# An attention and MLP kernel: the attention exps in two phases on either side of w3, the second q/k tile filled by DMA, all engine orders pinned

## The chip, the cores and the metric

The kernel runs on one core of one Trainium2 chip. The metric is device time in microseconds (us) of one execution; lower is better. Most executions of one kernel agree within 0.3%, but several kernels here fall into two groups about 2% apart, fast or slow (slow: more than 1.5% above the fastest of the same kernel), and comparisons use fast runs. The profile also gives the *granted clock* of TensorE: 1 is full speed, 0.5 is half.

A *ratio* in this text is the estimate of one kernel's time over that of the kernel before, from the fast runs of the same rounds on the same chip. It is not quite the ratio of the medians quoted beside it. Brackets give a 95% interval.

## The reference, cut to what matters

```python
# S = 2048 positions, D = 512, 32 heads of 16, F = 1376, bf16
x = A_x
xn = layernorm(x)
# A: each query sees 8 keys: itself and those 2, 4, ... 14 positions back
s = attention(xn @ wqkv, window=8, dilation=2) @ wo
# B: h = gelu(layernorm(xn) @ w1); its four column groups shifted by +1, -1, +2, -2 rows; then w2
x1 = xn + shifted(h) @ w2
b  = x1 + gelu(layernorm(x1) @ w3) @ w4
out = x + s * silu(b)
```

Positions fall into an even and an odd half (p = 0 and p = 1) of 1024; dilation 2 makes attention a dense window of 8 inside a half. Each half has nine *units* of up to 128 queries.

## The kernel before

The sliding window is imposed inside the score matmul. A score matmul reads 32 rows (partitions) of a key tile and of a query tile: 16 rows are one head, and 16 rows are *mask rows*, whose product adds a large negative number outside the window. Two tiles exist of each (e = 0 and 1), in which heads and mask rows change places. ScalarE writes the q/k rows into both tiles from the matmul's result, and then DMAs overwrite 16 of every 32 rows of each tile with mask rows out of a small table in memory.

```python
for a in range(ND):                             # stage_a2: QK
    ...                                         # 8 matmuls into pt
    for e in range(2):                          # the result goes into both tiles
        nc.scalar.activation(dst[e][:, n0 : n0 + 2, cs], pt, AF.Copy)

for w in range(2):                              # end of build_mask: the table goes to memory
    nc.sync.dma_start(out=mask_d[w].rearrange("r (g l) -> g r l", l=W), in_=rows[w])

def fill_mask(p, w):                            # w: 0 keys, 1 queries
    t = (kT[p], qT[p])[w]
    for e in range(2):
        for gr in range(4):
            r = 32 * gr + DH * (1 - e)          # 16 partitions, 128 KB
            pin(nc.sync.dma_start(out=t[e][r : r + DH, :, :],
                                  in_=mask_d[w].unsqueeze(1).to_broadcast([DH, ND, M])))
```

(`DH` is 16, `ND` 4, `M` 1024, and `pin` keeps an instruction in program order.) `nc.sync` is the queue of the SyncE engine, the only one that issues loads here. Each entry waits for what it needs; entries behind it wait with it. The order of the stages is:

```python
stage_ln(0) ... stage_a2(2)        # layer norm, transposes, QK and w1 of four chunks of 512
build_mask()
stage_b(0); stage_a2(3); stage_b(1); stage_b(2)   # w2, third layer norm, round trip through memory
stage_w3(0); stage_b(3)
fill_mask(0, 0); fill_mask(0, 1)
stage_w3(1); stage_w3(2); stage_w3(3)
# then 18 units of attention; each holds 11 w4 matmuls in its first eight,
# the rest of w4 and wo tiles later
```

`stage_b` ends with the *round trip*: the normalised x1 goes to memory and comes back transposed as `x1nT`, which w3 reads. After every third unit comes the chain of the *denominators*: the sums of the exps go to memory, come back (`dn`), VectorE takes the reciprocal (`rb`), it goes to memory (`rden_d`) and comes back spread out, and VectorE multiplies the attention output by it.

The softmax here doesn't subtract the row's maximum and nothing guards it: scores larger than these inputs give would overflow.

## Time and profile before

227.31 us, median of 3 runs (226.96 to 228.37).

| what | before |
|---|---|
| span of the profiled execution | 222.8 us |
| PE (TensorE matmul) busy | 205.6 us, 92% |
| ACT (ScalarE) busy | 136.2 us |
| first QK matmul | 10.06 us |
| waits for mask rows, 110 to 114 us | 3.1 us in four pieces |
| a unit of attention with 11 w4 matmuls | 4.78 us |

The following lines are from the page of the kernel before. The rows of digits cut the span into 40 slices of 5.6 us; each digit is the busy share (or, for PEclk, the granted clock) in tenths. The last line is the chain of work that ended last, by engine.

```profile
span 222.8 us, 4851 instructions
PE 205.6 (92%) x1992; PEld 95.3 (43%) x1992; DVE 130.1 (58%) x244; ACT 136.2 (61%) x158; POOL 61.9 (28%) x119
PE   8799999999999999999869999999969999999961
PEclk9999999999999999999988999999999999999998
DMA  5999100130390675799995005526650342625222
PE 67%; DMA 10%; DVE 8%; ACT 7%; POOL 2%; SPq 2%; issue 2%; DVEq 0%; ACTq 0%
```

TensorE is busy nearly everywhere. Two dents are visible before the end: one in the slices of 107 to 118 us, where the clock falls too, and a 6 in the slice of 161 to 167 us. DMA is 10% of the chain. The next lines are pieces of that chain (start, us, what):

```profile
97.31 7.99 DMA kT_155<-mask_d
105.32 8.73 DMA qT_159<-mask_d
```

And these are lines of TensorE's timeline there (start, us, engine, line, operation, tiles; in brackets the idle time just before and what ended it):

```profile
110.69 0.21 PE L461 MATMUL s_ps<-qT_159,kT_155 32*128 32x128 bf16 x1 [0.47 <-DMA qT_159<-mask_d]
111.90 0.21 PE L461 MATMUL s_ps<-qT_159,kT_155 32*128 32x128 bf16 x1 [0.99 <-DMA qT_159<-mask_d]
112.89 0.21 PE L461 MATMUL s_ps<-qT_159,kT_155 32*128 32x128 bf16 x1 [0.67 <-DMA qT_159<-mask_d]
114.08 0.21 PE L461 MATMUL s_ps<-qT_159,kT_155 32*128 32x128 bf16 x1 [0.98 <-DMA qT_159<-mask_d]
114.34 3.24 PE L413 MATMUL w_ps<-w_sb,h3T 128*128 128x512 bf16 x9
120.47 2.12 PE L413 MATMUL w_ps<-w_sb,h3T 128*128 128x512 bf16 x9
```

Four groups of scores wait for the four mask transfers one by one. Then nine matmuls take 3.24 us; nine at the full clock, 6 us later, take 2.12. (A duration shown here includes the end of the pipeline; the matmuls themselves follow each other every 0.2156 us.)

### The profile page before, as it was taken

Reading aid. Unit: us, or ns where it says so; the run is one execution under the profiler, and the core shown is the slowest. Engines: PE = TensorE matmul, PEld = TensorE weight load, DVE = VectorE, ACT = ScalarE, POOL = GpSimd, SP = SyncE. Lnnn points to the kernel's source line nnn. Section 1 sums busy time; section 2 is a strip of 40 time slices with the busy share of each in tenths; the row PEclk is TensorE's granted clock in tenths of the full one; section 3 lists DMA queues with packets and bytes.
Section 4 is the critical chain, followed back from the end, with each engine's and each line's share of the span. In section 5 each row is a group of like instructions: output and inputs, shape, how many; then the busy total and the mean of one; then the engine's idle time right before and its main releaser. Section 6 shows DMA issues by size and latency. Waiting matters only on the chain.

```text
span 222.8 us, 4851 instructions
## 1 busy us (share of the span) xinstructions
PE 205.6 (92%) x1992; PEld 95.3 (43%) x1992; DVE 130.1 (58%) x244; ACT 136.2 (61%) x158; POOL 61.9 (28%) x119
## 2 busy tenths in 40 slices
PE   8799999999999999999869999999969999999961
PEld 2335545444444444444323444444434445454420
DVE  6689964127279683000103566678457857795984
ACT  2086696956913615665457888898776978842110
POOL 1723563502002202000000007015074482947040
PEclk9999999999999999999988999999999999999998
DMA  5999100130390675799995005526650342625222
GB/s 160 371 392 388 47 0 4 4 8 0 122 161 3 171 195 154 170 118 121 119 122 60 0 3 119 157 68 159 209 125 13 101 83 70 154 51 148 67 85 94
DMA packets 32957, 25.60 MB, mean 115 GB/s; under 512 B 16152, under 2 KB 28792, under 8 KB 32936
## 3 DMA queue, kind: packets, MB, share of 16 engines
q1 hardware_dynamic: 30312, 22.16, 42.7%
q0 software_dynamic: 1536, 2.10, 4.9%
q10 hardware_dynamic: 1088, 1.05, 1.3%
q8 instruction: 15, 0.25, 0.5%
q14 instruction: 6, 0.05, 0.1%
HBM read 16.58 MB, written 4.52 MB: 95 GB/s over the span
## 4 chain that ended last, share of the span: by engine, by line
PE 67%; DMA 10%; DVE 8%; ACT 7%; POOL 2%; SPq 2%; issue 2%; DVEq 0%; ACTq 0%
PE w_ps L413 17%; PE qk_ps L317 9%; PE w_ps L392 9%; ACT prob L468 6%; PE w_ps L329 6%; PE w_ps L357 6%; PE s_ps L461 5%; PE v_ps L440 5%; PE wo_ps L573 4%; DMA qT_159<-mask_d 4%; DMA kT_155<-mask_d 4%; PE o_ps L489 3%; DVE l1s L253 2%; SPq L224 2%; DMA oT_1494<-orw 2%
## 5 line engine op out<-in xcount | busy, mean ns | idle before, releaser
L468 ACT ACTIVATE prob<-s_ps 128x960 bf16<-128x960 f32 (+2 forms) x72 | 62.7, 925 | 15.1 <-PE s_ps L461 14.1
L413 PE MATMUL w_ps<-w_sb,h3T 128*128 128x512 bf16 (+1 forms) x176 | 44.9, 390 | 0.0
L392 PE MATMUL w_ps<-x1nT,w_sb 128*128 128x512 bf16 (+1 forms) x176 | 38.3, 379 | 0.0
L397 ACT ACTIVATE h3T<-w_ps 128x1024 bf16<-128x1024 f32 x20 | 20.5, 1024 | 25.6 <-PE w_ps L392 23.3
L521 POOL DMA_DIRECT2D oT_1494<-orw x24 | 12.4, 523 | 68.2 <-DVE orw L496 68.2
L392 PEld LDWEIGHTS <-w_sb 128*128 128x128 bf16 (+1 forms) x176 | 17.6, 100 | 20.4
L413 PEld LDWEIGHTS <-h3T 128*128 128x128 bf16 (+1 forms) x176 | 15.1, 99 | 17.3 <-issue 1.0
L496 DVE CAST orw<-o_ps 128x960 bf16<-128x960 f32 (+2 forms) x18 | 19.7, 1098 | 1.3 <-PE o_ps L489 1.1
L445 DVE CAST v_aug_148<-v_ps 128x512 bf16<-128x512 f32 (+1 forms) x9 | 6.1, 682 | 23.0 <-PE v_ps L440 23.0
L317 PEld LDWEIGHTS <-wqk_sb 128*128 128x128 bf16 x128 | 12.1, 98 | 12.9
L317 PE MATMUL qk_ps<-xnT_152,wqk_sb 128*128 128x512 bf16 x64 | 15.3, 379 | 0.8 <-DVE xnT_152 L291 0.8
L420 DVE TENSOR_TENSOR xn_95<-w_ps,xn_95 128x512 bf16<-128x512 f32 x8 | 5.5, 684 | 16.5 <-PE w_ps L413 16.5
L329 PE MATMUL w_ps<-xn2T,w_sb 128*128 128x512 bf16 x64 | 14.6, 379 | 0.0
L317 PE MATMUL qk_ps<-xnT_153,wqk_sb 128*128 128x512 bf16 x64 | 14.5, 379 | 0.0
L584 POOL TENSOR_TENSOR xo_1715<-sg,xo_1715 128x512 bf16<-128x512 bf16 x8 | 10.4, 1297 | 14.5 <-DVE sg L582 13.4
L362 DVE TENSOR_TENSOR xn_95<-w_ps,xn_95 128x1024 bf16<-128x1024 f32 x4 | 4.9, 1215 | 14.4 <-PE w_ps L357 14.4
L422 ACT ACTIVATE sig<-xn_96 128x512 bf16<-128x512 bf16 x8 | 5.0, 630 | 12.6 <-DVE xn_96 L420 12.6
L521 POOL DMA_DIRECT2D oT_2418<-orw x24 | 12.1, 513 | 1.6 <-DVE orw L496 1.6
L246 POOL TENSOR_SCALAR l3r<-l3m 128x4 f32<-128x4 f32 x4 | 0.9, 232 | 36.7 <-DVE l3m L254 36.7
L440 PE MATMUL v_ps<-wv_sb,xnT_153 128*128 128x512 bf16 (+1 forms) x36 | 9.3, 380 | 2.0 <-DVE sg L582 2.0
L461 PE MATMUL s_ps<-qT_159,kT_155 32*128 32x120 bf16 (+2 forms) x144 | 7.7, 214 | 3.1 <-DMA qT_159<-mask_d 3.1
L573 PE MATMUL wo_ps<-wo_sb,oT_2418 128*128 128x512 bf16 x32 | 7.6, 379 | 2.2 <-DVE oT_2418 L545 2.2
(132 smaller groups left out, 329.3 us busy)
## 6 DMA issues: line engine op xcount, KB each, us to landing
w_sb<-in_B_w_dram SPq DMA_DIRECT2D x1, 1376.0 KB, 9.5
w_sb<-in_B_w_dram SPq DMA_DIRECT2D x1, 1280.0 KB
wqk_sb<-in_A_wqkv_dram SPq DMA_DIRECT2D x2, 512.0 KB
w_sb<-in_B_w_dram SPq DMA_DIRECT2D x2, 512.0 KB, 6.0
xn_96<-in_A_x_dram SPq DMA_DIRECT2D x4, 256.0 KB, 6.9
xo_1715<-in_A_x_dram SPq DMA_DIRECT2D x4, 256.0 KB, 5.5
xo_2325<-in_A_x_dram SPq DMA_DIRECT2D x4, 256.0 KB, 4.5
out_dram<-xo_1715 SPq DMA_DIRECT2D x4, 256.0 KB, 3.8
```

The lines of the kernel that those rows point to most:

```text
L317: nc.tensor.matmul(pt[:, b, :], lhsT=wqk_sb[:, dt, nt * P : (nt + 1) * P], rhs=xnT[p][:, dt, cs], start=(dt == 0), stop=(dt == ND - 1),)
L329: nc.tensor.matmul(pt[:, b, :], lhsT=w1_sb[:, dt, g * P : (g + 1) * P], rhs=xn2T[:, dt, :], start=(dt == 0), stop=(dt == ND - 1),)
L357: nc.tensor.matmul(pt[:, j, :], lhsT=w2_src(p, g, m0), rhs=w2_sb[:, g, :], start=(g == 0), stop=(g == ND - 1),)
L392: nc.tensor.matmul(pt[:fs, ft % 2, :], lhsT=w3_sb[:, dt, ft * P : ft * P + fs], rhs=x1nT[:, dt, :], start=(dt == 0), stop=(dt == ND - 1),)
L397: last["gelu"] = nc.scalar.activation(h3T[:, 2 * a : 2 * a + 2, :], pt, AF.Gelu_apprx_tanh)
L413: nc.tensor.matmul(pt, lhsT=h3[c][:fs, ft, jj * P : (jj + 1) * P], rhs=w4_sb[:fs, ft, :], start=(ft == 0), stop=(ft == NF - 1),)
L440: nc.tensor.matmul(vp[:nk, :], lhsT=xnT[p][:, dt, k0 : k0 + nk], rhs=wv_sb[:, dt, :], start=(dt == 0), stop=(dt == ND - 1),)
L461: nc.tensor.matmul(st[:nk, b, i * nq : (i + 1) * nq], lhsT=kT[p][e][r : r + 32, dt, k0 : k0 + nk], rhs=qT[p][e][r : r + 32, dt, q0 : q0 + ...
L468: nc.scalar.activation(prv[:nk, 2 * h : 2 * h + 2], st[:nk, :, 0 : 4 * nq], AF.Exp, scale=SCALE)
L496: nc.vector.tensor_copy(out=orw[p][:, :, :, q0 - ra : q0 - ra + nq], in_=op[:, :, 0 : 4 * nq].rearrange("p j (s q) -> p j s q", q=nq),)
L521: nc.gpsimd.dma_start(out=oT[p][DH * hh : DH * (hh + 1), :, ra : ra + rw], in_=orw[p][32 * cg : 32 * cg + DH, jj],)
L573: nc.tensor.matmul(pt[:, j, :], lhsT=oT[p][:, dt, (i + j) * P : (i + j + 1) * P], rhs=wo["sb"][:, dt, :], start=(dt == 0), stop=(dt == ND ...
```

## The change

Its intent is to spread ScalarE's exps, and to start attention earlier. The even half's nine units move in front of w3 (*phase 1*), interleaved with QK of the odd half and with w2; the odd half's nine units stay behind w3 (*phase 2*), interleaved with w4; all wo tiles go to the end. ScalarE no longer writes the second q/k tile; a DMA called `spread` copies the 16 head rows from tile 0 to tile 1 (partition to partition), and the mask rows of tile 0 can be filled only after it. The w4 load moves into the w3 stage. All five engines run in program order. The diff also puts nearly all tiles into one arena, halves the first layer norm's statistics and loads x ahead of w1, among other things. The core of the diff:

```diff
-            for e in range(2):
-                nc.scalar.activation(dst[e][:, n0 : n0 + 2, cs], pt, AF.Copy)
+            nc.scalar.copy(out=dst[:, n0 : n0 + 2, k * CH : (k + 1) * CH], in_=pt)
...
+    def spread(p, w):
+        t = (kT[p], qT[p])[w]
+        for gr in range(4):
+            r = 32 * gr + DH
+            nc.sync.dma_start(out=t[1][r : r + DH, :, :], in_=t[0][r : r + DH, :, :])
...
+    ctx.enter_context(tc.manual_schedule(engines={E.PE, E.Activation, E.DVE, E.Pool, E.SP}))
...
     build_mask()
+    for w in range(2):
+        fill_mask(0, w, 1)               # mask rows of tile 1: 8 transfers of 128 KB
...
+    for w in range(2):                   # after QK of chunk 1
+        spread(0, w)                     # 4 copies of 128 KB
+        fill_mask(0, w, 0)               # then 4 fills of tile 0
...
+    for n in range(N1):                  # phase 1: units of p = 0 with QK of p = 1 and w2
+        attend(n)
+    for c in range(NCH):                 # w3
+        for a in range((NF + 1) // 2):
+            w3_pair(c, a)
+            if c == 0 and a == 0:
+                weighted(*prev)()
+                prev = None
+                ln3_stats(2)
+                ln3_norm(2)              # round trip of chunk 2
+                ln3_stats(3)
+                ln3_norm(3)              # round trip of chunk 3
+                for w in range(2):
+                    spread(1, w)
+                    fill_mask(1, w, 0)
+                load_w4()
+                pack(0, 2)
+            if c == 1 and a == 0:
+                normalise_end(0, 1)
+                normalise_mid(0, 2)
+            if c == 2 and a == 0:
+                normalise_end(0, 2)
...
+    for n in range(N1, 2 * NU):          # phase 2: units of p = 1 with w4
+        attend(n)
```

## The prediction

> **What bounds the kernel now.** TensorE, and time in which it is starved. The page shows PE busy 205.6 of 222.8 us and PE as 67% of the chain that ended last. A full 128x512 matmul costs 0.2156 us of stream (timeline: 16 in 3.45 us); 744 of them are 160 us. Transposes add 3.5, 36 score groups about 18 (0.5 each), 18 weighted groups 9.5 (0.53 each): about 192 us that neither kernel avoids. The other 31 us are start (first QK matmul at 10.1), a hole at 16 to 17, and three places:
> - the mask fills: the chain has 16.7 us of mask DMA before the first exps; PE waits from 110 to 114, then runs at granted clock 0.5 to 0.7 (115 to 119 us; nine w4 matmuls take 3.2 us instead of 1.9);
> - the change of phase at 154 to 170 (exps, then the oT packing DMA, 3.55 us in the chain);
> - the end: last wo matmul at 216.4, end 222.8.
>
> In the middle, a unit of attention with 11 w4 matmuls takes 4.78 us, which is its PE work. ACT has 3.8 us of exps there (four of 0.967) and little else, but is idle half of the w3 stage.
>
> **What changes.**
> - PE work: the same matmuls, other order. No gain by itself.
> - ACT: 16 second q/k copies of 1.05 us go (17 us), none on the chain. Transpose evictions move to it (about 5 us). Two more table loads (1.28 us each).
> - DMA: 16 partition-to-partition copies, 2 MB. Fills of 512 KB take 4.39 us each now (119 GB/s, DMA share 1.1). The Trainium skill, "SBUF — State Buffer", Door 1, says DMA rate depends on the ports that the partitions reach; 16 partitions reach 4 of 16, an estimate of 109 GB/s from its 435. The trace agrees roughly.
> - Phase 1 (9 units, with 48 QK and 64 w2 matmuls): PE about 5.0 us a unit, ACT 3.9 + 0.8 of copies = 4.7. Coupled through two score banks: I expect 5.1 to 5.4.
> - Phase 2: 11 w4 matmuls a unit, 4.8 to 5.0. The wo tiles go to the end, where PE stays fed.
>
> **Sum (estimates from those durations).** First QK matmul about 8.3 (halved stats, x before w1). Then 36.5 of PE to the first scores, so about 45.5. Mask: rows ready about 24, then DMA fill 8.8, spread and fill of k, spread and fill of q, 13.5 to 17.5 more: ready 48 to 53. So PE waits 3 to 7 us again, now near 46, and pays about 1.5 of low clock. Phase 1: 47. w3: 38 + 1.5 for table loads. Phase 2: 45. Tail of w4 and wo: 28.5. Drain: 5.5. Span about 214; time is 4.5 more than the span as now: **218.5 us**, range 210 to 228. Chances: faster 0.73, same 0.20, slower 0.07.
>
> **What would show each step.** (1) first QK before 9 us; (2) the chain passes through the mask or spread DMA near 45 to 53, with one dip of the clock; (3) phase 1 at 5.1 to 5.4 us a unit, ACT over 85% busy; (4) w3 in 38 to 40 us without gaps; (5) phase 2 at 4.8 to 5.0; (6) no hole where packing is waited for; (7) PE over 95% busy from the first exp to the last matmul.
>
> **What would make it wrong.** The wait for spread and fill being over 10 us (a slower partition-to-partition copy, a late mask build): then 225 or more. Exps, QK copies and two shared banks locking step in phase 1 at 6 us a unit: 6 us more. VectorE falling behind in phase 1 or the tail. If the DMA is hidden wholly: 211.

## The result, and the profile after

The changed kernel takes **239.84 us** (median of 4 runs, 239.33 to 241.08) against 227.47 (226.96 to 228.37) for the kernel before: ratio 1.0626 [1.053, 1.0721], slower. The predicted time was 218.5 with a range of 210 to 228. Its page, the same parts (slices of 6.0 us):

```profile
span 238.6 us, 4930 instructions
PE 208.4 (87%) x1996; PEld 98.7 (41%) x1996; DVE 133.4 (56%) x244; ACT 129.7 (54%) x158; POOL 68.3 (29%) x137
PE   8889999605999999999998996299999999999870
PEclk9999999965799999999999999779999999999995
DMA  5981499669930164444287996878003050400632
PE 46%; DMA 29%; DVE 12%; SPq 5%; issue 3%; ACT 2%; POOL 1%; DVEq 0%; POOLq 0%
```

There are now two dents in the PE row, at about 42 to 60 us and 143 to 155 us, each with a dip of the clock, and DMA is 29% of the chain. The first dent in TensorE's timeline:

```profile
54.87 0.28 PE L484 MATMUL s_ps<-arena 32*128 32x128 bf16 x1 [9.32 <-DMA arena<-mask_d]
55.88 0.58 PE L484 MATMUL s_ps<-arena 32*128 32x128 bf16 x7 [0.73 <-DMA arena<-mask_d]
56.99 0.28 PE L484 MATMUL s_ps<-arena 32*128 32x128 bf16 x1 [0.53 <-DMA arena<-mask_d]
57.55 0.58 PE L484 MATMUL s_ps<-arena 32*128 32x128 bf16 x7 [0.28 <-DMA arena<-mask_d]
```

TensorE has finished all work before the first scores at 45.5 us and then waits 10.9 us in four pieces. The chain over that time (start, us, what; the pieces between, most of which issue the transfers, are left out) tells for what:

```profile
22.01 6.50 DMA mask_d<-m_rows
29.90 6.21 DMA arena<-mask_d
36.13 9.06 DMA arena<-arena
47.43 6.24 DMA arena<-arena
53.73 3.78 DMA arena<-mask_d
```

Mask table to memory, fills of tile 1, key copies, query copies, fills: 35.5 us from end to end, one after the other. (`arena` is the name of the one large tile that holds q, k, weights and more; `arena<-arena` is `spread`.) From the issue of the first fill at 28.58 to the last landing at 57.51 the queue moved 3 x 1,048,576 bytes, which is 109 GB/s.

The windows view shows the clock. The columns are the stretch, its length, five engines' busy time with instruction counts, and then PEclk, the DMA share and GB/s:

```profile
46.00:47.00 1.00, 0.00 (x0) 0.00 (x0) 0.00 (x0) 0.68 (x1) 0.00 (x0) 1.00 0.91 186
50.00:51.00 1.00, 0.00 (x0) 0.00 (x0) 0.00 (x0) 0.00 (x0) 0.00 (x0) 0.50 0.45 57
62.00:63.00 1.00, 1.00 (x4) 0.33 (x3) 0.39 (x1) 0.00 (x0) 0.00 (x0) 0.50 1.08 135
64.00:65.00 1.00, 1.00 (x20) 0.56 (x20) 0.70 (x2) 0.49 (x1) 0.00 (x0) 1.00 1.06 133
```

The clock is halved from about 49.4 us, 3.9 us after TensorE ran dry (49.4 is worked out from the mean of 0.70 in the window from 49 to 50), and comes back at 63.1, some 5.5 us after it had work again. The twelve w2 matmuls in that stretch take 5.2 us; in e10 below, at full clock, they take 2.84.

The second dent follows w3:

```profile
147.46 0.23 PE L484 MATMUL s_ps<-arena 32*128 32x128 bf16 x1 [1.02 <-DMA arena<-mask_d]
148.33 0.56 PE L484 MATMUL s_ps<-arena 32*128 32x128 bf16 x7 [0.64 <-DMA arena<-mask_d]
149.60 0.22 PE L484 MATMUL s_ps<-arena 32*128 32x128 bf16 x1 [0.70 <-DMA arena<-mask_d]
150.35 0.38 PE L484 MATMUL s_ps<-arena 32*128 32x128 bf16 x7 [0.53 <-DMA arena<-mask_d]
153.97 5.90 PE L438 MATMUL w_ps<-arena 128*128 128x512 bf16 x16 [3.25 <-DMA arena<-in_B_w_dram]
```

Scores wait for the odd half's mask rows, then w4 waits 3.25 us for its own weights, and its first sixteen matmuls take 5.90 us; in e15 below, at full clock, they take 3.63. The chain (again with pieces left out) says why the weights are late:

```profile
118.37 2.96 DMA x1n_dram<-arena
121.35 5.88 DMA arena<-x1n_dram
132.34 5.49 DMA arena<-arena
140.64 5.64 DMA arena<-arena
146.69 0.42 SPq L143
```

L143 is the w4 load, issued at 146.69 although its target was free from about 108 us, when VectorE had last read what lay there: it stood in the one queue behind two round trips, the copies and the fills, each of which waited for the one before. The Trainium skill, "DMA: Bandwidth & Descriptors", Anatomy of one DMA, states that a semaphore wait happens on the issuing sequencer before dispatch (its section follows a DMA of GpSimd's queue, but that sentence is about the DMA engines in general); this trace, of SyncE's queue, agrees: the SyncE queue's own waits between 115 and 150 us include 6.2 us for `x1n_dram<-arena`, 6.1 for `arena<-arena` and 3.7 for `den_d<-orw`.

Stage by stage, from the timeline:

| stage | predicted | after | what differs |
|---|---|---|---|
| first QK matmul | 8.3 | 8.59 | |
| first scores could start | 45.5 | 45.5 | |
| first scores after that | +3 to 7, then about 1.5 of low clock | +9.3; all mask rows in at 57.5, clock low until 63 | first dent: phase 1 ends at 106.55 and so takes 61.0; without a dent it takes 46.5 (measured in the last version below), so the dent cost 14.5 |
| phase 1, a later unit | 5.1 to 5.4 | 5.03 | |
| w3 | 39.5 | 39.9 | |
| first w4 | no hole | hole | second dent: phase 2 takes 55.0; without a dent 45.65 (the same version), so the dent cost 9.4 |
| phase 2, one unit | 4.8 to 5.0 | 4.95 | |
| tail, drain | 28.5, 5.5 | 30.0, 7.1 | |

The two dents are 23.9 us of the 238.6. Without them the span would be about 214.7; as the 46.5 and 45.65 come from e15, whose own span is 214.7, this is a way to share out the difference and not an independent check. In w3 the match with the prediction is partly luck: 39.9 includes a wait of 1.14 us for a round trip, and e15's w3 takes 38.8, so the 1.5 us for table loads did not show. Part of the tail may be VectorE, for which TensorE waits there 0.64 and 0.66 us; that the slower gate causes these waits is not shown. The gate's `SCALAR_TENSOR_TENSOR` averages 926 ns against 685 to 691 before. The one that started at 212.58 took 1.62 us, while a GpSimd add ran from 212.51 to 213.66; it ended 0.54 us after that add. The Trainium skill, "SBUF — State Buffer", on the shared port pair, says that VectorE and GpSimd exclude each other there for a whole instruction; the trace agrees.

### The profile page after: what moved, and what is told of

Its sections match the earlier page's. It is cut to its first block, busy times and chain, and to the rows that moved or that the text cites. A ratio compares the mean times of both kernels' runs of the same rounds, so it can differ in the third digit from the quotient of the medians.

```text
span 238.6 us, 4930 instructions
## 1 busy us (share of the span) xinstructions
PE 208.4 (87%) x1996; PEld 98.7 (41%) x1996; DVE 133.4 (56%) x244; ACT 129.7 (54%) x158; POOL 68.3 (29%) x137
## 3 DMA queue, kind: packets, MB, share of 16 engines
q1 hardware_dynamic: 30760, 24.26, 46.5%
## 4 chain that ended last, share of the span: by engine, by line
PE 46%; DMA 29%; DVE 12%; SPq 5%; issue 3%; ACT 2%; POOL 1%; DVEq 0%; POOLq 0%
PE w_ps L438 14%; DMA arena<-arena 11%; PE w_ps L384 7%; PE v_ps L464 6%; PE s_ps L484 6%; PE qk_ps L348 4%; DMA arena<-mask_d 4%; PE o_ps L507 3%; PE wo_ps L585 3%; DMA mask_d<-m_rows 3%; DMA rden_d<-rb 3%; DMA arena<-x1n_dram 2%; SPq L222 2%; DMA arena<-in_A_x_dram 2%; DVE arena L591 2%
## 5 line engine op out<-in xcount | busy, mean ns | idle before, releaser
L489 ACT ACTIVATE arena<-s_ps 128x960 bf16<-128x960 f32 (+2 forms) x72 | 63.2, 934 | 27.8 <-PE s_ps L484 27.8
L438 PE MATMUL w_ps<-arena 128*128 128x512 bf16 (+1 forms) x176 | 44.2, 394 | 3.3 <-DMA arena<-in_B_w_dram 3.2
L546 POOL DMA_DIRECT2D arena<-orw x48 | 24.9, 526 | 73.5 <-DVE orw L519 62.4
L484 PE MATMUL s_ps<-arena 32*128 32x120 bf16 (+2 forms) x576 | 19.9, 213 | 14.4 <-DMA arena<-mask_d 13.8
L423 ACT ACTIVATE arena<-w_ps 128x1024 bf16<-128x1024 f32 x20 | 20.5, 1024 | 16.9 <-PE w_ps L418 16.9
L438 PEld LDWEIGHTS <-arena 128*128 128x128 bf16 (+1 forms) x176 | 17.1, 100 | 24.4 <-issue 6.7
L388 DVE TENSOR_TENSOR arena<-w_ps,arena 128x512 bf16<-128x512 f32 x16 | 11.0, 688 | 27.9 <-PE w_ps L384 27.9
L418 PEld LDWEIGHTS <-arena 128*128 128x128 bf16 (+1 forms) x176 | 17.4, 100 | 21.6 <-DMA arena<-x1n_dram 1.6
L418 PE MATMUL w_ps<-arena,arena 128*128 128x512 bf16 (+1 forms) x88 | 19.3, 379 | 1.1 <-DMA arena<-x1n_dram 1.1
L418 PE MATMUL w_ps<-arena 128*128 128x512 bf16 (+1 forms) x88 | 19.5, 379 | 0.0
L464 PE MATMUL v_ps<-wv_sb,arena 128*128 128x512 bf16 (+1 forms) x72 | 18.6, 380 | 0.2 <-DVE arena L444 0.2
L384 PE MATMUL w_ps<-arena 128*128 128x512 bf16 x64 | 18.6, 426 | 0.0
L332 PE MATMUL qk_ps<-arena 128*128 128x512 bf16 (+1 forms) x96 | 18.3, 344 | 0.0
L361 PE MATMUL w_ps<-arena 128*128 128x512 bf16 x64 | 14.5, 379 | 0.0
```

The source lines that it names most:

```text
L332: nc.tensor.matmul(pt[:, b, hh * w : (hh + 1) * w], lhsT=wqk_sb[:, dt, nt * P : (nt + 1) * P], rhs=xnT[p][:, dt, k * CH + hh * w : k * CH ...
L384: nc.tensor.matmul(pt, lhsT=w2_src(p, g, m0), rhs=w2_sb[:, g, :], start=(g == 0), stop=(g == ND - 1))
L418: nc.tensor.matmul(pt[:fs, ft % 2, :], lhsT=w3_sb[:, dt, ft * P : ft * P + fs], rhs=x1nT[c][:, dt, :], start=(dt == 0), stop=(dt == ND - 1),)
L423: nc.scalar.activation(h3T[c][:, 2 * a : 2 * a + 2, :], pt, AF.Gelu_apprx_tanh)
L438: nc.tensor.matmul(pt, lhsT=h3T[c][:fs, ft, jj * P : (jj + 1) * P], rhs=w4_sb[:fs, ft, :], start=(ft == 0), stop=(ft == NF - 1),)
L464: nc.tensor.matmul(vp[:nk, :], lhsT=xnT[p][:, dt, k0 : k0 + nk], rhs=wv_sb[:, dt, :], start=(dt == 0), stop=(dt == ND - 1),)
```

## The experiments

Eighteen runs. Theory **A** says that the loss is only the two dents: chains of transfers that land late, plus the low clock that follows. Its sub-theory **A1** says that the alternation of copies and fills makes the first chain slow, and **P** that the ports under 16 partitions do. Rivals say that the new order of work (locked-step units, ScalarE, other engines) costs time itself, or, for the second dent, that a wait taken away just returns elsewhere. All edits are against the changed kernel unless a line says otherwise.

### The first dent

**e1_no_spread: without the copies (the result is wrong).**

```diff
-   lhsT=kT[p][e][r : r + 32, ...], rhs=qT[p][e][...]
+   lhsT=kT[p][0][r : r + 32, ...], rhs=qT[p][0][...]   # both heads read tile 0
-        spread(0, w)
-                    spread(1, w)
```

> The 16 partition-to-partition copies are left out and both score operands are read from the first tile of each pair, so the result is wrong on purpose; all matmuls, exps and mask fills stay. Theory A (the copies, and the mask fills queued behind them, make both holes of TensorE): fills of the first half end about 45 (36.1 plus 8.8 us of the remaining fills), so the wait at 45.4 falls from 9.3 us to under 2 and the clock stays at 1.0; the second hole at 147 to 154 goes too, because the queue reaches the w4 load about 140. Time 215 to 220. Rival B (the 4 MB of mask fills and the late mask rows alone make the holes): the first wait stays above 7 us, time 232 or more. Rival C (in the second hole it is the w4 load's place, not the copies): the second hole stays.

Measured: 223.37 us median, fast runs 220.23 to 221.0, ratio 0.9789 [0.9666, 0.9912]. The fast runs lie below the kernel before, but the verdict on record is unclear: half of the runs are slow. Three of six runs were at 225.7 to 226.4 with a clock of 0.973 to 0.978, against 0.99 for the fast ones. The profile caught a slow one, and no fast one has a trace; in the slow one the first wait is four short pieces, 1.99 us together as expected, but the clock falls all the same, which was not expected:

```profile
46.85 0.38 PE L484 MATMUL s_ps<-arena 32*128 32x128 bf16 x7 [0.72 <-DMA arena<-mask_d]
49.65 4.47 PE L384 MATMUL w_ps<-arena 128*128 128x512 bf16 x10 [0.22 <-issue]
```

Ten w2 matmuls in 4.47 us are half rate. At the second boundary waits of 0.91 us for w4 and 2.33 us for VectorE are left. So taking the copies out takes most of the loss away, and a stutter of about 2 us, in which no gap is longer than 0.72, can go with the low clock; that was seen in a slow run here, and in a fast one of the kernel before. The fills alone still moved 2 MB between 27.9 and 48.3, 103 GB/s.

**e3_keep_warm: idle matmuls in the dents.**

```diff
+    keep_warm(42)                                        # ahead of the first scores
+    keep_warm(16)                                        # ahead of the first scores of phase 2
+    groups[N1][0].insert(0, lambda: keep_warm(14))       # between these and w4
```

> 42 idle matmuls of 128x512 before the first scores and 16 + 14 around the first scores of the second phase, so TensorE works while it waits; the waits themselves stay. Theory: after the first hole TensorE runs at clock 0.5 for about 6 us of work (12 w2 matmuls in 5.1 us instead of 2.6) and after the second likewise (16 w4 in 5.8 instead of 3.45); with no idle time the clock stays at 1.0 and the kernel gains 5 to 8 us: 232 to 235. Rival (the low clock is not caused by idling, or it only hides in other waits): 239 to 241.

Measured: 234.28 us, ratio 1.0375 [1.0267, 1.0484], clock 0.996, span 231.8. The waits stay nearly as long, now filled with idle matmuls (the last of the first scores starts at 56.02 instead of 57.55, and from the end of w3 to the first w4 matmul it is 6.94 us instead of 7.53), and the clock does not fall: fifteen w4 matmuls after the second dent take 3.62 us, where sixteen took 5.90. The difference of the two ratios, 1.0626 and 1.0375, is 5.7 us of 226, but each has an interval of 0.01 on either side, and the waits were a little shorter too. A count from the changed kernel's trace gives less: TensorE worked 5.5 us at half the clock after the first dent and 4.65 after the second, which costs half of that, 5.1 us. So about 5 us of the loss is low clock, and the rest is waiting.

**e2_spread_first: both copies, then both fills.**

```diff
     for w in range(2):
         spread(0, w)
+    for w in range(2):
         fill_mask(0, w, 0)                # the same for p = 1
```

> Only the order of issue on the DMA queue: both copies of a half, then both fills, instead of copy, fill, copy, fill. The result is right. Theory A1 (the fill waits in the queue for the copy before it to land, and keeps the next copy waiting behind it): the score wait shrinks by the two bubbles seen at 44 to 46 and 50 to 54, from 9.3 us to 4 to 7, and the second hole by 2 to 4; time 232 to 236. Rival (only the bytes count): no change, 239 to 241.

Measured: 238.98 us, ratio 1.0564 [1.0442, 1.0687]; the first wait is 7.46 us instead of 9.32. The expectation was missed: the alternation costs 1.9 us of the 9.3, not the dent. A1 falls as the main cause.

**e8_two_queues: half of the row groups on GpSimd's queue.**

```diff
-        spread(0, w)
-        fill_mask(0, w, 0)
+        spread(0, w, (0, 1))
+        fill_mask(0, w, 0, (0, 1))
+    for w in range(2):
+        spread(0, w, (2, 3), nc.gpsimd)      # row groups at partitions 64 to 127
+        fill_mask(0, w, 0, (2, 3), nc.gpsimd)
```

> Copies and fills of row groups 2 and 3 go out from GpSimd's queue, those of groups 0 and 1 stay on the sync queue; same bytes. Result right. Theory P (the rate of 105 to 115 GB/s is that of the few SBUF ports that one 16-partition transfer reaches, as the Trainium skill, SBUF - State Buffer, Door 1, has it: groups 0 and 1 reach other ports than 2 and 3): two transfers run side by side, the rate over 36 to 57 rises to 150 or more, the first scores come at 50 or before instead of 54.9, time 230 to 235. Rival E (the engines' own rate for these shapes, or the row reads from memory): rate unchanged at 105 to 120, first scores within 1.5 us of 54.9.

Measured: 244.77 us, ratio 1.0865 [1.0708, 1.1022]; the first waits are 9.02 and then 4.56 us. Two queues at once, on two sides of the partitions, moved a mean of 125 GB/s from 33 to 55 us, where the one queue of the changed kernel moved 123. Nothing is gained, and the second wait is new: part of it is that other loads now stood ahead in the SyncE queue. P in the form it was stated falls: other ports in parallel do not add rate. The skill's page "SBUF — State Buffer" says this too, which the expectation overlooked: under "Can I just issue two DMAs to hit both halves?" it answers no, since two transfers at once gained it 6%. Its Door 1 table gives 104 GB/s for 16 partitions; 103 to 119 here agree. That a transfer over 16 partitions runs at this rate is thus seen and agrees with the page; which part of the hardware sets it is not shown by these runs.

**e4_act_copies: ScalarE writes the second tile again (one part undone).**

```diff
-                nc.scalar.copy(out=dst[:, n0 : n0 + 2, ...], in_=pt)
+                for e in range(2):
+                    nc.scalar.copy(out=dst[e][:, n0 : n0 + 2, ...], in_=pt)
-        spread(0, w)
```

> Undoes one part of the change: the second q/k tile is written by a second copy on ScalarE again, and all mask fills of a half follow the last copy. Theory A: the first wait falls to 2 to 5 us (16 fills of 128 KB at 119 GB/s from 29.5 end about 47), but ScalarE gets 7 us more in phase 1, so its units take 5.4 to 5.7 us instead of 5.03; the second hole stays near 6 us, since 16 fills stand before the w4 load. Time 229 to 235. Rival B (fills alone are the cost): 239 or more.

Measured: 235.57 us, ratio 1.0365 [1.0222, 1.0509] (the profile is of a slow run). The first dent shrinks to 0.25 + 0.93 + 0.36 + 0.41 us of waits; the second stays and grows (waits of 4.85 us together for mask rows instead of 2.89, then 3.23 for w4), and a stretch of low clock stays after the first. So undoing the DMA copies removes most of the first wait and none of the second dent. This is still slower than the kernel before; but the edit also puts all sixteen fills of the odd half into w3, ahead of the w4 load, so it does not say by itself how much is left without the copies. Phase 1's units took 5.1 to 5.3 us, under the expected 5.4 to 5.7.

**e7_mask_early: the mask table computed at the start.**

```diff
+    m_tab = mask_tables()               # before the first layer norm
     ln_stats(0, 0, 2)
...
     ln_again(0)
+    build_mask(m_g)                     # in GpSimd's idle time
-    build_mask()                        # was after stage_t(1, 1)
```

> The mask rows are computed at the start: tables before the first layer norm, the rest in GpSimd's idle time after it. Result right. Theory (the first hole is the length of a chain of 16-partition transfers at 105 to 115 GB/s that begins when the rows have been written to memory, 28.5): rows written about 20, the first fills done by 29.5, copies start when the QK evictions are done, so the chain ends 6 to 7 us earlier, the score wait falls from 9.3 to 2 to 4 us, the low clock may go; second hole unchanged. Time 229 to 234. Rival (the chain is held by its order of waits or by the copies' own start, not by the mask): less than 3 us gained, 237 or more.

Measured: 233.41 us, ratio 1.0372 [1.0286, 1.0459], as expected. The table's two writes are issued at 13.0 and 15.1 instead of 22.0 and 24.2, and the fills start at 22.65 instead of 28.58; the first waits are 1.37 + 0.87 + 0.70 + 0.42, and the last of the first scores starts 6.5 us earlier. A stretch of half clock follows still, and the second dent is unchanged. So the late start of the chain is one of its causes; how much of it the 6.5 us write of the table is, apart from the rows themselves, this run does not separate.

**e10_first_halves: the columns of the first 512 queries first.** The first units of attention read only the first columns. The p = 0 copies and fills are cut in two, first half as soon as QK of chunk 0 is done:

```diff
-    def spread(p, w):
+    def spread(p, w, cols=slice(0, M)):
...
     stage_t(1, 1)
+    for w in range(2):
+        spread(0, w, HALF[0])
+    for w in range(2):
+        fill_mask(0, w, 1, HALF[0])
+    for w in range(2):
+        fill_mask(0, w, 0, HALF[0])
...                                        # the same with HALF[1] after QK of chunk 1
```

> For the first half of the rows (p = 0) the copies and fills are split by columns: 64 KB each, first the 512 columns that attention units 0 to 3 read, then the other 512. Same bytes, twice as many transfers; everything else as in the changed kernel. Result right. Theory (TensorE waits at the first scores only because the first unit waits for bytes that units 4 to 8 need): the first columns need 1.5 MB after 24 to 29, about 14 us at 110 GB/s, so they are there by 43 to 45; the score wait falls from 9.3 to under 2 us and the low clock of the first hole goes; the second columns land by 58, before unit 4 at 65. Second hole unchanged. Time 224 to 229. Rival (smaller transfers are slower, or the units wait for the whole tile): wait over 6 us, 236 or more.

Measured: 227.01 us, ratio 1.0112 [1.0046, 1.0178]; span 225.7. The first dent is gone; between the first scores and w3 no wait is over 0.3 us. The first line below shows the first scores, which wait for nothing; what is left is the second dent:

```profile
46.05 0.42 PE L487 MATMUL s_ps<-arena 32*128 32x128 bf16 x16
134.40 0.22 PE L487 MATMUL s_ps<-arena 32*128 32x128 bf16 x1 [2.27 <-DMA arena<-mask_d]
140.85 6.24 PE L441 MATMUL w_ps<-arena 128*128 128x512 bf16 x16 [3.06 <-DMA arena<-in_B_w_dram]
```

The same bytes at the same rate, earlier by 12.9 us of span. Theory A holds for the first dent.

### The second dent

Here everything hangs on the order of the one queue in the w3 stage: two round trips, two denominator chains, 1 MB of copies, 1 MB of fills and the w4 load.

**e6_w3_order: the w4 load and the copies ahead of the round trips.**

```diff
                 weighted(*prev)()
+                load_w4()
+                for w in range(2):
+                    spread(1, w)
                 ln3_stats(2)
                 ...
-                load_w4()
```

> Only the order on the DMA queue in the w3 stage: the w4 load and the four-by-two copies of the second half go before the layer-norm round trips, the fills between the two. Result right. Theory (the second hole is the queue's order: the copies stood behind the last round trip until 130, the w4 load behind the fills until 147): the copies start at 107, the w4 load lands by 115, fills end by 140; no wait between w3 and w4, clock 1.0 there; the first hole is unchanged. Gain 8 to 10 us: 229 to 232. Rival (the transfers are too slow to fit into the w3 stage wherever they stand, or they delay the round trips so that w3 waits): 236 or more.

Measured: 248.97 us, ratio 1.1044 [1.0942, 1.1146]: worse, and a miss. The wait moved to w3:

```profile
142.44 11.55 PE L418 MATMUL w_ps<-arena,arena 128*128 128x512 bf16 x43 [15.40 <-DMA arena<-x1n_dram]
```

(The profile is of a slow run.) The queue stood at the reading of the denominators until 118.8, so the copies came at 120.0 and the round trips after them.

**e9_combined: e7, e2, e6 and five early w2 tiles together.**

> Early mask rows, both copies of a half before its fills, the w3 stage's new queue order, and five w2 tiles moved ahead of the first scores, with part of the third block's statistics moved into phase 1. Result right. Theory (two DMA holes and their low clock are all that separates the changed kernel from what its TensorE order allows): no wait over 2 us at the first scores nor between w3 and w4, clock over 0.98; time 214 to 220, faster than the kernel before by 3 to 6%. Rival (removing the holes shows another limit, such as phase 1 bound by ScalarE or a late layer norm): 222 or more.

Measured: 240.75 us, ratio 1.0695 [1.0617, 1.0773]. The first dent is gone, and w3 waits 16.6 us for a round trip, as in e6.

**e11_halves and e12_halves_early: the p = 1 copies into phase 1.** e11 is e10 and these lines; e12 adds the early mask table and half of the third layer norm's statistics in phase 1.

```diff
+        late[2].append(lambda w=w: spread(1, w, HALF[0]))
+        late[4].append(lambda w=w: fill_mask(1, w, 0, HALF[0]))
+    late[6].append(lambda: spread(1, 1, HALF[1]))
+    late[7].append(lambda: fill_mask(1, 1, 0, HALF[1]))
+                        late[8].append(load_w4)
```

> As the run with first halves, and for p = 1 too: copies and fills by columns inside phase 1, when the DMA engines are idle, as soon as their QK columns are evicted; only the last quarter stays in the w3 stage, behind the layer-norm round trips; the w4 load goes out at the end of phase 1. Result right. Theory: neither hole is left, clock over 0.98, phase 1 still 5.0 to 5.1 us a unit, w3 in 38 to 41; time 214 to 219, 3 to 5% faster than the kernel before. Rival (the earlier run that moved the copies forward stalled w3 by 15 us behind them; if the round trips again queue behind copies, w3 waits): 224 or more, with the wait at x1nT.

> As the run before, with the mask rows computed at the start and half of the third block's layer-norm statistics in phase 1. Result right. Theory: the first columns are ready 5 us earlier than needed, so small remaining waits at the first scores and at the third block of w3 (1.1 us) go: 1 to 2 us faster than the run before, 213 to 218. If the statistics overload VectorE in phase 1, no gain.

Measured: e11 231.34 us, ratio 1.0292 [1.0243, 1.0342]; e12 228.11, ratio 1.0163 [1.0108, 1.0218]. Neither waits for mask rows or w4 any more. But the third of w3's four blocks now waits for its round trip, 9.76 us in e11 (which has two more waits of 2.0 us in w3) and 7.42 in e12: the round trip stood behind the denominators' waits (issued at 119 and 113.5).

**e14_trips_first: e10, with the round trips first, then w4, copies, a denominator chain and fills.**

```diff
                 ln3_norm(3)
-                for w in range(2):
-                    spread(1, w); fill_mask(1, w, 0)
-                load_w4()
+                load_w4()
+                for w in range(2):
+                    spread(1, w)
+                normalise_mid(0, 1)              # was in phase 1
+                for w in range(2):
+                    fill_mask(1, w, 0)
...                                              # the multiplications of w3 each one block later
```

> As the run with first halves (225.9 to 228.8 us), with another order in the w3 stage alone: both layer-norm round trips before the denominators of runs 1 and 2, then the w4 load, then both copies, the denominators of run 1, both fills. Result right. Theory Q (the queue's order): the round trips are issued by about 101 and 106 instead of 104 and 109 to 114, the copies start by 112 instead of 116, the w4 load no longer stands last, so the wait of 3 us for it goes and the scores' wait falls under 3; time 218 to 223. Rival V (2 MB of copies and fills at 110 GB/s are too much for the stage): the score wait at the second phase stays at 4 us or more; 224 or more.

Measured: 231.87 us, ratio 1.0253 [1.0181, 1.0326]. No wait in w3 and none for w4; instead the first scores of phase 2 wait 9.81 us, which the profile puts down to the denominators' write, and then 1.2 us for mask rows. The fills stood behind that chain in the queue: they were issued at 129.3 to 136.3, and the last landed at 143.4. Moving the order alone does not do it. That the stage is too short for all the copies in it is a reading of this; the bytes and the waits of the denominators were not separated.

**e13_best: e12, with the round trips ahead of the denominators and the w4 load after them.** Now both ideas together: part of the copies in phase 1, and the queue in the order of need.

```diff
+                load_w4()                        # after ln3_norm(3)
                 spread(1, 0, HALF[1])
+                normalise_mid(0, 1)
                 fill_mask(1, 0, 0, HALF[1])
-                        late[8].append(load_w4)
-            if c == 1 and a == 0:                # normalise_end(0, 1), normalise_mid(0, 2)
+            if c == 2 and a == 0:
-            if c == 2 and a == 0:                # normalise_end(0, 2)
+            if c == 3 and a == 0:
```

> As the run with early halves, with the round trips before the denominators in the queue and the w4 load behind them. Result right. Theory Q: x1nT of the third and fourth block land before w3 reaches them (needed at about 116 and 126), no wait over 1 us in w3 nor between w3 and w4; clock over 0.985; span 215 to 218, time 216 to 221, faster than the kernel before by 2 to 4%. Rival: another chain (w4 or the last copies) makes a hole of over 3 us: 223 or more.

Measured: 226.79 us median of 4 (223.71 to 228.02), ratio of the fast runs 0.9929 [0.9825, 1.0032]; the profile is of a slow run. One wait over 2 us is left:

```profile
138.95 0.42 PE L494 MATMUL s_ps<-arena 32*128 32x128 bf16 x16
144.63 1.87 PE L474 MATMUL v_ps<-wv_sb,arena 128*128 128x512 bf16 x4 [5.26 <-DVE arena L454]
146.28 2.43 PE L448 MATMUL w_ps<-arena 128*128 128x512 bf16 x6
```

TensorE waits for VectorE to empty a bank, and VectorE, in program order, stood at the multiplication by denominators whose transfer landed only then. The w4 load is there in time. This slow run also stops for 1.58 us at 63.4 for nothing that the profile shows, with a stretch of half clock after it; e15 has no such stop. So the gain from e13 to e15 is to be read from the fast times: 223.7 to 226.3 there against 216.6 to 218.9.

**e15_late_scaling: e13, with that multiplication moved to where it is free.**

```diff
-            if c == 2 and a == 0:
-                normalise_end(0, 1)
-                normalise_mid(0, 2)
-            if c == 3 and a == 0:
-                normalise_end(0, 2)
                 pack(0, 2)
+                normalise_mid(0, 2)
...
+    late[9].append(lambda: normalise_end(0, 1))     # phase 2, first unit
+    late[11].append(lambda: normalise_end(0, 2))    # phase 2, third unit
```

> Edit against e13: the two multiplications of the first half's attention output by its denominators (runs 1 and 2) move from w3's third and fourth blocks into the first and third unit of phase 2, and the reciprocal of run 2 into w3's first block; nothing else. Theory A (the loss of the changed kernel is only waits at the two boundaries and the low clock that follows them; the order of the work itself is worth the predicted gain): e13's last wait over 1 us (5.26 us at 139.4 to 144.6, VectorE standing at a multiplication whose denominators had not landed) goes, the clock stays above 0.98, w4's first sixteen matmuls take under 3.7 us, span 216 to 220 and 217 to 222 us, below the kernel before by 2 to 4%. Rival R (the boundary's transfers are more than w3's stage holds, so that a wait removed returns elsewhere): a wait of 3 us or more appears on another tile between 105 and 150, and the time stays at 224 to 228.

Measured: **218.31 us**, median of 6 (216.59 to 220.44), against 226.83 for the kernel before; ratio 0.9658 [0.9606, 0.9709]. The result is correct. Its page and its timeline at the place of the second dent:

```profile
span 214.7 us, 4969 instructions
PE   8778999999999999999999999999999999999850
PEclk9999999999999999999999999999999999999997
```

```profile
131.94 0.71 PE L494 MATMUL s_ps<-arena 32*128 32x128 bf16 x16
132.58 3.63 PE L448 MATMUL w_ps<-arena 128*128 128x512 bf16 x16
136.15 0.42 PE L494 MATMUL s_ps<-arena 32*128 32x128 bf16 x16
```

No wait is left between w3 and phase 2, the first sixteen w4 matmuls take 3.63 us, and the clock is 0.994. This is what theory A expected, or slightly better (span 216 to 220, time 217 to 222), and the rival's wait elsewhere did not come.

**e15_again: the same kernel again, on the chip of the next control.**

> The same kernel as e15_late_scaling, beside the repaired kernel before on one chip. If its gain is real, the ratio repeats at 0.960 to 0.972, and it stays below b1 by 1 to 2%. If the first result owed to that chip, the ratio is over 0.975.

Measured: 217.05 us (216.26 to 217.45) against 224.94; ratio 0.9636 [0.9579, 0.9693]. It repeats.

### Control: the same repair in the kernel before

The kernel before has a dent of its own, so part of e15's gain may be that dent and not the order of work. Three edits **of the kernel before** try to take it away.

**b1_before_fill_early** issues its first fills earlier:

```diff
     stage_a2(3)
+    fill_mask(0, 0)
+    fill_mask(0, 1)
     stage_b(1)
     ...
     stage_b(3)
-    fill_mask(0, 0)
-    fill_mask(0, 1)
```

> The kernel before, with one edit: its first mask fills (16 transfers of 128 KB) are issued before the second w2 stage instead of after the last. In the kernel before the hole at 110 to 114 costs 3.1 us of waiting and about 2.2 us of low clock (nine w4 matmuls in 3.24 us). Theory C (that hole too is only late transfers): the wait on mask rows goes, span about 218 and time about 222 us, ratio 0.975 to 0.985, and the gain of e15 is then about half its holes and half its order of work. Rival D: the fills collide with the layer-norm round trips of w3, a wait of over 1 us on x1nT appears, and the ratio stays within 1% of 1.

Measured: 231.05 us, ratio 1.0276 [1.021, 1.0341]. No scores wait for mask rows, but w3 waits for a round trip that now stood behind the fills:

```profile
90.18 30.15 PE L392 MATMUL w_ps<-x1nT,w_sb 128*128 128x512 bf16 x132 [7.93 <-DMA x1nT<-x1n_dram]
```

**b2_before_halves** leaves the place and splits the fills by columns, as e10 does:

```diff
-    fill_mask(0, 0)
-    fill_mask(0, 1)
+    for cols in HALF:
+        fill_mask(0, 0, cols)
+        fill_mask(0, 1, cols)
```

> The kernel before, with the repair that removed the changed kernel's first hole (e10): at the same place in the queue, its first mask fills go by columns, first the 512 columns that the first units read, then the rest; twice as many transfers of half the size. Theory C: the first half lands 6 to 8 us sooner than the last fill did (114 us), so the four waits on mask rows (3.1 us) and the low clock after them (about 2.2 us) go: span 217 to 219 and ratio 0.970 to 0.985; the order of work of the repaired changed kernel (0.9636 to 0.9658) is then worth 1 to 2% by itself. Rival D: something else holds the boundary (as in b1, where the wait moved to x1nT) and a wait of over 2 us appears on another tile; ratio 0.99 to 1.01.

Measured: 231.55 us, ratio 1.0219 [1.0166, 1.0273]. The dent at 110 to 114 is gone. But the scheduler, which is free in this kernel, now issues the reading of the first denominators at 145.35 instead of 137.63, and the wait is back:

```profile
163.23 0.99 PE L493 MATMUL o_ps<-prob,v_aug 128*32 128x120 bf16 x32 [12.07 <-DVE orw L500]
```

**b3_before_halves_pinned** is b2 with the SyncE queue in program order:

```diff
+    ctx.enter_context(tc.manual_schedule(engines={mybir.EngineType.SP}))
     stage_ln(0)
```

> b2 (the kernel before with its mask fills split by columns), and in addition all transfers of the one queue are issued in program order, as the changed kernel has them; b2 had left that to the scheduler, which put the reading of the first denominators at 145.4 instead of 137.6 us and so made a new wait of 12.1 us. Theory C: both waits are gone, the clock is above 0.985, span 215 to 218 and ratio 0.965 to 0.980, so that at most about 1% of the repaired changed kernel's gain (0.9636 to 0.9658) belongs to its order of work. Rival D: a wait of over 2 us appears on yet another tile and the ratio is 0.99 or more; then what the order alone is worth stays open.

Measured: 238.06 us, ratio 1.0527 [1.0467, 1.0586]; a wait of 9.4 us on VectorE at the same tile, and a new one of 3.3 us for packed output at the end. All three were missed, each in the way its rival named: the wait moved. b1 and b2 came out even slower than their rivals' ranges, which were within 1% of the kernel before. So it stays **open** how much of e15's gain the order of work gives by itself. What is shown is that the changed order, once its queue is in order, beats the kernel before by 3.4 to 3.6%, and that in either kernel most repairs of this queue only move its wait.

## Why the prediction was wrong

- *"First QK matmul about 8.3", "36.5 of PE to the first scores, so about 45.5"*: right, 8.59 and 45.5.
- *"Phase 1 ... 5.1 to 5.4", "w3: 38 + 1.5", "Phase 2 ... 4.8 to 5.0"*: right or slightly cautious; 5.03, 39.9 (in part by luck, see above) and 4.95. Units did not lock step. The picture of the work on the engines held. Two of the signs it named did not show: ScalarE was busy 81% of phase 1 (34.1 of 42.0 us, from 64 to 106 us), not over 85%, and TensorE 94% from the first scores to the last matmul (165.6 of 176.6 us), not over 95%.
- *"ready 48 to 53"*: the step that failed first. The last mask rows were in at 57.5. The terms of the sum as they stand give 46.3 to 50.3; measured, the rows were in memory at 28.5 instead of 24, the fills of tile 1 took 7.5 us (until 36.1) instead of 8.8, and the copies and fills 21.4 more instead of 13.5 to 17.5. The next two points are these terms.
- *"Mask: rows ready about 24, then DMA fill 8.8"*: a missing term. The rows are indeed computed about 24, but they must first be written to memory, which is 32 KB per tile in runs of 16 bytes: issued at 22.0 and 24.2, done at 28.5, 4.5 us after the 24. The sum had no term for it. In e7, where the fills start 5.9 us earlier, the last of the first scores start 6.5 us earlier.
- *"spread and fill of k, spread and fill of q, 13.5 to 17.5 more"*: the term that was mis-sized. The prediction had itself quoted 109 GB/s as an estimate for 16 partitions. At that rate, 2 MB take 19.2 us, and 3 MB 28.9, which is what was measured (28.58 to 57.51). That the match is exact is partly luck, since the stretch holds waits too: 37 GB/s from 44 to 45 us, and e2 gains 1.9 us by order alone. The sum's 13.5 to 17.5 us mean 120 to 155 GB/s: the upper time is just four of the 4.39 us fills that the kernel before had shown, with nothing for waits between copies and fills, and the lower one no line of the profile had shown.
- *"PE waits 3 to 7 us again ... and pays about 1.5 of low clock"*: it waited 10.9 us, and with the low clock the dent cost 14.5. The prediction had named this branch: a wait over 10 us, *"then 225 or more"*.
- *"no hole where packing is waited for", "with one dip of the clock"*: wrong; a second dent of 9.4 us, and a second dip. This is the second step that failed, by omission. The DMAs of the w3 stage were taken as hidden because their sum is short; but they are one queue in program order, with waits inside it. e6, e11 and e14 move the wait to a round trip or to the denominators; e13 and e15 take it away by order and place.
- Low clock: about 5 us in both dents together (the trace; e3 agrees within its interval), where the sum had 1.5.
- *"Tail 28.5. Drain: 5.5"*: 30.0 and 7.1, partly VectorE beside GpSimd adds.
- *"time is 4.5 more than the span as now"*: for one and the same execution it is 1.8 to 2.5; the profiled one of before was a quick one. The changed kernel's median is only 1.2 over its profiled span. This erred the other way.

The prediction's stages add up to 211 and its span was 214, so it held about 3 us for the first dent. The terms together: 11.5 more there (14.5 less 3), 9.4 for the second dent, 3.1 in tail and drain, 0.6 in the other stages, less 3.3 of offset (4.5 less 1.2), which is the 21.3 us by which it missed. *"If the DMA is hidden wholly: 211"* does not say whether it is a span or a time; it was too low either way: e15, where hardly any wait for DMA is left, has a span of 214.7 and takes 217 to 218.

## What to carry to other kernels

When a change moves work onto a DMA queue, write down that queue's timetable as one would an engine's: every entry in program order, with its wait, its bytes at the rate that *this* shape showed, and the landing that some engine needs; a queue that is short in sum can still be late, since an entry that waits holds back everything behind it. Deliver first what is read first (here the first 512 columns). A load whose source and target are free need not stand behind chains that wait, but what is read sooner still goes before it: e6 put the w4 load and the copies ahead of the round trips, and w3 waited 15.4 us. Let no in-order engine stand at a result that is not needed yet. Count a starved TensorE at more than its wait: here another 2 to 3 us per dent went to the low clock, and it also fell after a row of short waits, in the kernel before and in a slow run of e1.

## What the Trainium skill lacked or had wrong

- "TensorE: Matmul & The Clock Gate", Part 1 and its summary advise against idle gaps over about 3 us. The page also tells of a kernel whose many short idle times between matmul groups made the clock oscillate, but gives no figure for how low the activity must be. In the kernel before no gap was over 0.99 us, but TensorE was only 10 to 43% busy from 110 to 114 us, and the clock fell to 0.5 from 115.2 to 118.6; in a slow run of e1 four waits of at most 0.72 us came before the fall. A single gap of 1.96 us in the kernel before, at 165 to 167 us, did not lower it.
- The same page gives about 3.4 us of work to get the full clock back, and says that the clock is set by a free-running window of 3413 ns. The traces agree with the window: worked out from the clock means of 1 us stretches, the clock is low for 3.41 us (before, from 115.18), 6.83 (after, from 151.80; e1; e13), 10.24 (e10), 13.65 (after, from 49.40) and 17.07 (e8), all whole multiples of 3.413, and the two falls in the changed kernel are 102.40 us apart, which is 30 of them. So the time from the first steady work to the full clock is not a constant: 3.6 us (e13), 4.5 (before), 4.6 (after, second dent) and 5.5 (after, first dent); the drop came 2.1 us (e13) to 3.9 us (after) after the last matmul. Whether the window also makes the two groups of runs of e1 (clock 0.99 or 0.975) is not shown.
- The same page calls the penalty of the ramp at the start under 1% of a typical span. Two dents in the middle cost 2 to 2.5% here (5.1 us of 226 by the changed kernel's trace, 5.7 by e3).
- "SBUF — State Buffer", Door 1: the rate for 16 partitions agrees (104 there, 103 to 119 GB/s here), and so does the answer that two transfers at once do not add (e8). It has no figure for copies from partition to partition; here copies of 128 KB, issued in fours, landed a median of 7.5 us after issue, against 5.4 us for fills of the same size from memory. That does not show copies to be slower, since it counts the time behind earlier transfers: from 20 to 60 us both medians are 7.5.
- "DMA: Bandwidth & Descriptors", Specifications, asks for at least 512 bytes a run. It has no figure for what a small transfer in short runs takes; here two of 32 KB in runs of 16 bytes, issued 2.2 us apart, took 6.5 us until both had landed.
- No page gives a worked example of one issuing queue with waits inside it, though the page on DMA states where the wait happens. Here the w4 load went out at 146.69 us, though its target was free from about 108.
